# An attention and mixture-of-experts kernel: the first expert's weights loaded a group earlier, the k copies moved to ScalarE, the router two slots earlier

## The chip, the cores and the metric

The kernel runs on one core of one Trainium2 chip. A time is the device time of one execution in microseconds (us). The kernel before was run five times: 498.47, 499.37, 502.02, 503.82 and 508.04 us, median 502.02 us.

## What is computed

Two stages follow each other. The first is block-causal attention: 8 batches, 8 heads, 576 positions, head size 64. A query sees all keys of its own block of 64 positions and of the blocks before it. The second is a mixture of 8 experts on the 4608 rows that the attention gives, each row 512 wide.

```python
scores = scale * q @ k.T                       # masked by blocks of 64 positions
attn = softmax(scores)
x = (attn @ v) -> rows [4608, 512]             # heads side by side

noisy = x @ w_gate + log1p(exp(x @ w_noise)) * noise
top2 = two largest of 8 per row;  top2_w = softmax of those two
for e in range(8):
    for k in range(2):
        rows = top2[:, k] == e
        out[rows] += top2_w[rows, k] * (relu(x[rows] @ w1[e]) @ w2[e])   # w1 512x1024, w2 1024x512
```

## The kernel before

**Attention in groups and slots.** The batches are worked on in four groups of two (g = 0 to 3). A group has 26 score units (UG = 26), and a unit is one slot of a schedule written out by hand: `at(slot, fn, ...)` hangs a piece of work on a slot, and `run(u)` emits what hangs on slot u after the unit's own score matmuls (L288, L299) and their exponential on ScalarE (L291, L302). Each engine does its instructions in the order in which they are emitted. Two PSUM buffers hold scores (`sc_ps`), two the attention outputs and the router's products (`av_ps`), two the transposes (`tr_ps`).

- `load_qk` (L200, L202), `load_v` (L210): rows of q, k and v, fp32 in memory and bf16 in SBUF, by GpSimd's DMA queue.
- `transpose_qk`: TensorE transposes a chunk of q or k into PSUM (L250, L252), and VectorE copies it to SBUF: q at L255 in straight order, k at L257 with a strided read, since the columns of k are wanted in token order. A group has six k chunks: four of 128x1024 and two of 64x512. After chunk 0 VectorE also copies one block of 64 columns within SBUF (L261).
- `av_tile`: the product with v (L325, L336), and its division by the sum on VectorE (L339, L340) into `xr`.
- `x_transpose` (L354, copied at L355), then `router`, a chain of 15 steps: logits (L365), an exponential and a logarithm on ScalarE (L369 to L371), the two largest of eight on VectorE (L375 to L395), ranks by a scan (L399 to L406), two matmuls for the counts (L411, L412, into an `av_ps` buffer) and the row's place in its expert's list (L416 to L456). The slots of the steps are in the list `rsl`.
- `scatter`: 18 indirect DMAs per group, on GpSimd (L474), that write each row of `xr` to two places of the table `xd[half]`. Groups 0 and 1 make half 0, groups 2 and 3 half 1. They start at slot `r1` after the group's end.

The work of a group's second part runs beside the scores of the next group. For group 3 it runs beside the first steps of the expert stage.

**Experts.** `SEQ` lists 16 batches b of (half, expert), each of up to 640 rows: first half 0 of experts 0 to 3, then half 1 of experts 0 to 3, then both halves of experts 4 to 7 in turn. `load_x` (L493) loads a batch's rows transposed by a DMA of the sync engine's queue (SP): into `xa` for b = 0, into one of three `xg` buffers after that. It waits for all 36 scatters of its half. `load_rec` (L500) loads what the router wrote beside each row. `layer1` (L548, Relu at L551) and `layer2` (L560) follow; the product of layer 2 goes, scaled, to a table in memory (L565, L566), or is added to the row that was gathered from there (`gather`, L587; L569) and scattered to the output (L571).

**Queues.** SP's queue does, in order: the noise, eight DMAs that clear part of `xd[0]`, eight that clear part of `xd[1]` (`clear_x`, L619, each held back until the exponential of a named slot), `load_x(0)`, `load_rec(0)`, `load_x(1)`, `load_x(2)`, and then writes and loads of the experts. GpSimd's queue does all other transfers in order: rows of q, k and v, scatters, weights and gathers. The DMAs of this queue take eight completion semaphores in turn, and each waits until the DMA eight places before it has landed. Weights come from `load_w`: with k = 0 to 3 it loads half of w1 (k = 0, 1) or half of w2 (k = 2, 3) of one expert, 512 KB each as bf16 (L227). The schedule of this part is, in the kernel before:

```python
at(3 * UG + 12, load_x, 0)
at(3 * UG + 12, load_rec, 0)
...
at(UG + 4, clear_x, 0, UG + 3)
at(3 * UG + 4, clear_x, 1, 3 * UG + 3)
for k in range(4):
    at(3 * UG + (2, 5, 8, 11)[k], load_w, wE, 0, k)
    at(3 * UG + (14, 17, 20, 23)[k], load_w, wE, 1, k)
```

Of the kernel before, what the change touches and what calls it, by code (L numbers as in the profile page):

```python
# [11 lines left out]
AF = mybir.ActivationFunctionType  # L12
# [7 lines left out]
def kernel(  # L20
# [12 lines left out]
    nc = tc.nc  # L33
# [30 lines left out]
    UG = 2 * UN  # L64
# [32 lines left out]
    wE = main.enter_context(tc.tile_pool(name="wE", bufs=2))  # L97
# [132 lines left out]
    def transpose_qk(g, nm, ch):  # L230
        dst = qT if nm == "q" else kT
        tp = tr_ps.tile([P, 1024], BF16, tag="tr")


        if ch in (0, 1, 2, 3):
            raw = raws[(g, nm, ch)]
            p0, p1, c0, nb = 0, P, ch * 1024, 16
        else:
            raw = raws[(g, nm, 4)]
            p0 = 0 if ch == "4A" else 64  # L240
            p1, c0, nb = p0 + 64, 4 * 1024, 8
        n = nb * 64
        if nm == "q":
            to = tp[:, 0:n].rearrange("p (b r j) -> p b r j", b=nb, r=8)
        else:
            to = tp[:, 0:n].rearrange("p (r b j) -> p b r j", b=nb, r=8)
        for r in range(8):
            if nb == 16:
                for hf in range(2):
                    nc.tensor.transpose(to[64 * hf:64 * hf + 64, :, r, :], raw[:, hf, r * 64:(r + 1) * 64], ident)  # L250
            else:
                nc.tensor.transpose(to[p0:p1, :, r, :], raw[p0:p1, 0, r * 64:(r + 1) * 64],  # L252
                                    ident[p0:p1, p0:p1])
        if nm == "q":
            nc.vector.tensor_copy(dst[p0:p1, c0:c0 + n], tp[p0:p1, 0:n])  # L255
        else:
            nc.vector.tensor_copy(dst[p0:p1, c0:c0 + n].rearrange("p (b j r) -> p b j r", b=nb, j=8),  # L257
                                  tp[p0:p1, 0:n].rearrange("p (r b j) -> p b j r", r=8, b=nb))
        if ch == 0:

            nc.vector.tensor_copy(dst[64:128, 72 * 64:73 * 64], dst[64:128, 0:64])  # L261
# [343 lines left out]
    def at(slot, fn, *args):  # L605
        todo.setdefault(slot, []).append((fn, args))
# [75 lines left out]
    for ch in ("4B", 0):  # L682
        for nm in "qk":
            transpose_qk(0, nm, ch)
    at(0, transpose_qk, 0, "q", 1)
    at(0, transpose_qk, 0, "k", 1)

    for g in range(NG):
        s0 = g * UG
        if g + 1 < NG:  # L690
            early = 5 if g else 0
            at(s0 + 13 - early, transpose_qk, g + 1, "q", "4B")
            at(s0 + 13 - early, transpose_qk, g + 1, "k", "4B")
            at(s0 + 13, transpose_qk, g + 1, "q", 0)
            at(s0 + 15, transpose_qk, g + 1, "k", 0)
            at(s0 + 24, transpose_qk, g + 1, "q", 1)
            at(s0 + 25, transpose_qk, g + 1, "k", 1)
            at(s0 + 18, load_qk, g + 1, (2, 3))
            at(s0 + 11, load_v, g + 1)
        if g + 2 < NG:  # L700
            at(s0 + 20, load_qk, g + 2, (4, 0, 1))
        at(s0 + 3, transpose_qk, g, "q", 2)
        at(s0 + 5, transpose_qk, g, "k", 2)
        at(s0 + 10, transpose_qk, g, "q", 3)
        at(s0 + 12, transpose_qk, g, "k", 3)
        at(s0 + 17, transpose_qk, g, "q", "4A")
        at(s0 + 18, transpose_qk, g, "k", "4A")
        for i in range(TG):
            at(s0 + UN + 2 + i, av_tile, g, 0, i)
        r0 = s0 + UG  # L710
        if g < 2:
            for i in range(TG):
                at(r0 + 1 + i, av_tile, g, 1, i)
            for j in range(5):
                at(r0 + min(4 + 2 * j, 11), x_transpose, g, j)
            rsl = [12, 13, 14, 15, 16, 17, 18, 19, 20, 21, 21, 22, 22, 23, 23]
            r1 = 24
        elif g == 2:
            for i in range(TG):
                at(r0 + 1 + 2 * i // 3, av_tile, g, 1, i)  # L720
            for j in range(5):
                at(r0 + (3, 5, 6, 7, 8)[j], x_transpose, g, j)
            rsl = [9, 9, 10, 11, 12, 13, 14, 14, 15, 16, 16, 17, 17, 18, 18]
            r1 = 19
        else:
            for i in range(TG):
                at(r0 + i // 2, av_tile, g, 1, i)
            for j in range(5):
                at(r0 + 2 + j, x_transpose, g, j)
            rsl = [7, 7, 8, 9, 9, 10, 11, 11, 12, 13, 13, 14, 14, 15, 15]  # L730
            r1 = 16
        for j in range(RSTEPS):
            at(r0 + rsl[j], router_step, g)
        for j in range(2 * TG):
            at(r0 + r1 + (2 * j // 3 if g else j), scatter, g, j)
    at(3 * UG + 12, load_x, 0)
    at(3 * UG + 12, load_rec, 0)
    at(6, setup_consts)
    at(7, sort_nz, 0)
    at(8, transpose_nz, 0)  # L740
    at(9, sort_nz, 1)
    at(11, transpose_nz, 1)
    at(UG + 4, clear_x, 0, UG + 3)
    at(3 * UG + 4, clear_x, 1, 3 * UG + 3)
    for k in range(4):
        at(3 * UG + (2, 5, 8, 11)[k], load_w, wE, 0, k)
        at(3 * UG + (14, 17, 20, 23)[k], load_w, wE, 1, k)
    for u in range(NG * UG):
        score_unit(*divmod(u, UG))
        run(u)  # L750
# [61 lines left out]
    with tc.If(rs["over"] > 0):  # L812
# [4 lines left out]
        for g in range(NG):  # L817
# [5 lines left out]
            for idx in range(TG):  # L823
                for p0, tok in token_blocks(g, idx):
                    nc.sync.dma_start(out=token_order(tok_w[tok:tok + 64, :]), in_=wd[p0:p0 + 64, g, idx, :])
                    nc.sync.dma_start(out=token_order(tok_s[tok:tok + 64, :]),
                                      in_=slots[p0:p0 + 64, g * TG + idx, 0:1])
        for half in range(NH):
            with tc.For_i(half * TH * P, (half + 1) * TH * P, P) as r0:
# [6 lines left out]
                    out=xo.bitcast(I32), out_offset=None, in_=xd[half].bitcast(I32),  # L836
                    in_offset=bass.IndirectOffsetOnAxis(ap=sidx, axis=0),
                    bounds_check=XR - 1, oob_is_err=False)
                tp = tr_ps.tile([P, 1024], BF16, tag="tr")
# [53 lines left out]
```

## Time and profile before

| What | Value |
|---|---|
| median of five runs | 502.02 us |
| the profiled execution: its time, its span in the trace | 498.71 us, 496.8 us |
| granted TensorE clock, mean over the span | 0.902 of full speed |
| TensorE matmuls busy (PE) | 421.4 us, 85% |
| ScalarE busy (ACT) | 238.5 us, 48% |
| VectorE busy (DVE) | 182.6 us, 37% |
| GpSimd busy (POOL, its DMA issues among it) | 252.8 us, 51% |
| first matmul of the experts (L548) starts at | 176.72 us |

How to read it: the profile is of one execution. The span runs from its first to its last instruction; the rest of the 498.71 us lies around it. Times of single instructions are counted from the span's start. A busy TensorE is not a TensorE at its peak, since matmuls overlap. PE is the TensorE matmul, PEld its weight load, SPq the sequencer of the sync engine that issues DMAs. A group of instructions is named by its source line, engine, operation and tiles (out<-in). "Idle before" is the time in which the engine had nothing to do just ahead of the instruction, and the arrow tells what it then waited for. Busy shares are averages over two unlike stages: up to about 165 us attention, then the experts.

### The profile page before, as it was taken

The page shows a single profiled execution, that of the slowest core. Times are in us where ns is not written, and L with a number is a line of the kernel's source. Part 1 is how long each engine was busy: PE and PEld are TensorE (multiplying, and loading weights), DVE is VectorE, ACT ScalarE, POOL GpSimd, SP SyncE. Part 2 cuts the span into 40 slices and gives each one's busy share as a digit, 9 for nine tenths or more (in the row PEclk, how much of TensorE's full clock was granted, in tenths as well). Part 3 has the DMA queues.
Part 4 walks back from the last instruction along what each step waited for, and adds up shares of the span by engine and source line. Part 5 has one row for each costly group of instructions (what it writes and reads, how often), then busy time and mean ns, then how long its engine had stood idle before and what let it go on. Part 6 is the DMA issues. An engine that isn't in the chain of part 4 may idle for free.

```text
span 496.8 us, 9869 instructions
## 1 busy us (share of the span) xinstructions
PE 421.4 (85%) x3936; PEld 258.8 (52%) x3952; DVE 182.6 (37%) x552; ACT 238.5 (48%) x319; POOL 252.8 (51%) x297
## 2 busy tenths in 40 slices
PE   3788968988868279998383999999989999999994
PEld 2456645664635156555151556655645655665561
DVE  3687898788876238300100301011011022023112
ACT  1658776566475114545050545545535554554330
POOL 8775384786785253277330301234452463475553
PEclk9959997778875579999695999999999999999999
DMA  8999999399779999957696586887999984695232
GB/s 134 162 136 148 206 144 170 107 114 145 192 177 181 155 157 211 211 142 200 149 155 102 128 186 128 159 157 186 143 215 192 216 222 113 138 184 178 81 119 96
DMA packets 134763, 78.68 MB, mean 158 GB/s; under 512 B 96130, under 2 KB 124548, under 8 KB 134709
## 3 DMA queue, kind: packets, MB, share of 16 engines
q0 software_dynamic: 70496, 55.79, 74.2%
q1 hardware_dynamic: 64212, 22.18, 22.8%
q8 instruction: 33, 0.54, 0.5%
q14 instruction: 22, 0.17, 0.1%
HBM read 68.28 MB, written 33.13 MB: 204 GB/s over the span
## 4 chain that ended last, share of the span: by engine, by line
PE 30%; issue 25%; POOL 14%; DMA 14%; DVE 14%; ACT 1%; POOLq 1%; ACTq 0%; DVEq 0%
PE yp L560 11%; PE hp L548 10%; POOL yg L587 5%; DMA xa<-xd 5%; POOL out_dram L571 5%; DMA xd<-xr,slots 4%; PE tp L250 3%; DVE hq L257 3%; DVE xr L340 2%; DMA xg<-xd 2%; POOL xd L474 2%; PE sc L288 2%; PE av L325 2%; DMA yg<-yd,orow 2%; PE av L336 1%
## 5 line engine op out<-in xcount | busy, mean ns | idle before, releaser
L560 PE MATMUL yp<-w2sb,hq 128*128 128x512 bf16 x624 | 144.0, 386 | 13.1 <-DVE yo L569 11.6
L548 PE MATMUL hp<-xg,w1sb 128*128 128x320 bf16 x960 | 134.2, 300 | 8.7 <-DMA xg<-xd 8.7
L548 PEld LDWEIGHTS <-w1sb 128*128 128x128 bf16 x1024 | 100.6, 99 | 62.1 <-DMA xd<-xr,slots 11.3
L551 ACT ACTIVATE hq<-hp 128x640 bf16<-128x640 f32 x128 | 90.1, 704 | 89.0 <-PE hp L548 89.0
L569 DVE SCALAR_TENSOR_TENSOR yo<-yp,wrow,yg 128x512 f32<-128x512 f32 x46 | 34.4, 751 | 248.8 <-ACT ysb L565 181.5
L291 ACT ACTIVATE esc<-sc 128x1024 bf16<-128x1024 f32 x96 | 94.3, 1025 | 60.7 <-PE sc L288 59.7
L560 PEld LDWEIGHTS <-hq 128*128 128x128 bf16 x640 | 63.4, 99 | 89.4 <-issue 21.0
L474 POOL DMA_INDIRECT xd<-xr,slots x72 | 71.5, 993 | 53.5 <-issue 14.9
L571 POOL DMA_INDIRECT out_dram<-yo,trow x46 | 46.6, 1014 | 96.6 <-DVE yo L569 88.7
L565 ACT ACTIVATE ysb<-yp,wrow 128x512 bf16<-128x512 f32 x70 | 48.1, 687 | 90.7 <-PE yp L560 90.7
L587 POOL DMA_INDIRECT yg<-yd,orow x46 | 47.2, 1026 | 52.0 <-ACT hq L551 40.4
L288 PE MATMUL sc<-hq 64*128 64x512 bf16 (+4 forms) x320 | 44.0, 350 | 5.1 <-ACT esc L291 3.5
L325 PE MATMUL av<-vt,esc 128*128 128x65 bf16 x640 | 36.5, 215 | 11.5 <-DVE xr L340 10.0
L325 PEld LDWEIGHTS <-esc 128*128 128x128 bf16 x640 | 28.9, 111 | 25.3 <-DVE xr L340 14.5
L210 POOL DMA_DIRECT2D vt<-in_v_dram x40 | 33.7, 872 | 13.5 <-PE av L336 8.5
L340 DVE TENSOR_TENSOR xr<-av,rden 128x256 bf16<-128x256 f32 x72 | 30.6, 424 | 2.5
L250 PE MATMUL tp<-ident,t 128*64 128x128 bf16 x512 | 26.2, 262 | 2.2 <-DMA t<-in_q_dram 2.0
L257 DVE COPY hq<-tp 128x1024 bf16<-128x1024 bf16 (+1 forms) x24 | 25.6, 1066 | 4.3 <-PE tp L250 3.6
L250 PEld LDWEIGHTS <-t 128*64 128x64 bf16 x512 | 20.2, 135 | 7.7 <-issue 3.8
L339 DVE RECIPROCAL rden<-av 128x4 f32<-128x4 f32 x72 | 12.6, 175 | 30.1 <-PE av L325 21.5
L548 PE MATMUL hp<-xa,w1sb 128*128 128x320 bf16 x64 | 11.2, 325 | 11.2 <-DMA xa<-xd 11.2
L288 PEld LDWEIGHTS <-hq 64*128 64x128 bf16 x320 | 12.3, 100 | 15.5 <-issue 8.3
(126 smaller groups left out, 239.4 us busy)
## 6 DMA issues: line engine op xcount, KB each, us to landing
yd<-ysb SPq DMA_DIRECT2D x70, 128.0 KB, 2.4
w1sb<-in_moe_w_dram POOLq DMA_DIRECT2D x12, 512.0 KB, 6.8
w2sb<-in_moe_w_dram POOLq DMA_DIRECT2D x12, 512.0 KB, 9.1
t<-in_q_dram POOLq DMA_DIRECT2D x16, 256.0 KB, 7.3
t<-in_k_dram POOLq DMA_DIRECT2D x16, 256.0 KB, 8.0
vt<-in_v_dram POOLq DMA_DIRECT2D x32, 128.0 KB, 7.9
xd<-zero SPq DMA_DIRECT2D x16, 132.0 KB, 4.6
w1sb<-in_moe_w_dram POOLq DMA_DIRECT2D x2, 1024.0 KB, 10.5
```

The lines of the kernel that those rows point to most:

```text
L250: nc.tensor.transpose(to[64 * hf:64 * hf + 64, :, r, :], raw[:, hf, r * 64:(r + 1) * 64], ident)
L288: nc.tensor.matmul(out=sc[:, hf, off:off + z - a], lhsT=kT[sl, c0 + jt * P:c0 + jt * P + P], rhs=qT[sl, c0 + a:c0 + z], start=True, stop=True)
L291: ins = nc.scalar.activation(out=esc[:, hh, :, piece * 512:(piece + 1) * 512], in_=sc, func=AF.Exp, scale=scale)
L325: nc.tensor.matmul(out=av[:, hh, :], lhsT=esc[:, hh, hf, c:c + P], rhs=vb[:, 4 * hf + jt, h, :], start=(jt == 0), stop=(jt == ib))
L340: nc.vector.tensor_tensor(out=xr[:, idx, st * SET * D:(st + 1) * SET * D].rearrange("p (h d) -> p h d", h=SET), in0=av[:, :, 0:D], in1=rde ...
L474: ins = nc.gpsimd.indirect_dma_start(out=xd[half].bitcast(I32), out_offset=bass.IndirectOffsetOnAxis(ap=slots[:, g * TG + idx, i:i + 1], a ...
L548: nc.tensor.matmul(out=hp[:, n, 0:NW], lhsT=w1sb[:, db, fb * P:(fb + 1) * P], rhs=xgs[b][:, db, n * NW:(n + 1) * NW], start=(db == 0), sto ...
L551: ins = nc.scalar.activation(out=hs[b][:, fb, :].rearrange("p (n w) -> p n w", n=2), in_=hp[:, :, 0:NW], func=AF.Relu)
L560: nc.tensor.matmul(out=yp, lhsT=hs[b][:, fb, c * P:(c + 1) * P], rhs=w2sb[:, fb, :], start=(fb == 0), stop=(fb == FB - 1))
L565: nc.scalar.activation(out=ysb, in_=yp, func=AF.Copy, scale=w)
L571: ins = nc.gpsimd.indirect_dma_start(out=out, out_offset=bass.IndirectOffsetOnAxis(ap=trow[half][:, e, c:c + 1], axis=0), in_=yo, in_offse ...
L587: ins = nc.gpsimd.indirect_dma_start(out=yg, out_offset=None, in_=yd[half][0:e * CAP, :], in_offset=bass.IndirectOffsetOnAxis(ap=orows[hal ...
```

## The change

Four edits of the schedule and one of an engine.

- The copy of a k chunk out of PSUM (L257) is an activation with the function Copy on ScalarE in place of a copy on VectorE.
- The router steps of groups 0 and 1 are drawn together and end two slots earlier, and their scatters start two slots earlier (`r1` 24 becomes 22). In group 2 four steps move forward by one slot; its `r1` stays.
- The weights of expert 0 are hung on slots 4, 6, 8, 10 of group 2 in place of 2, 5, 8, 11 of group 3; those of expert 1 one slot earlier in group 3.
- `load_x(0)` moves from slot 12 to 11 of group 3, `load_rec(0)` from 12 to 14.
- The clears of half 1 move from slot 4 of group 3 to slot 4 of group 2.

```diff
         if nm == "q":
             nc.vector.tensor_copy(dst[p0:p1, c0:c0 + n], tp[p0:p1, 0:n])
         else:
-            nc.vector.tensor_copy(dst[p0:p1, c0:c0 + n].rearrange("p (b j r) -> p b j r", b=nb, j=8),
-                                  tp[p0:p1, 0:n].rearrange("p (r b j) -> p b j r", r=8, b=nb))
+            nc.scalar.activation(out=dst[p0:p1, c0:c0 + n].rearrange("p (b j r) -> p b j r", b=nb, j=8),
+                                 in_=tp[p0:p1, 0:n].rearrange("p (r b j) -> p b j r", r=8, b=nb), func=AF.Copy)
...
-            rsl = [12, 13, 14, 15, 16, 17, 18, 19, 20, 21, 21, 22, 22, 23, 23]
-            r1 = 24
+            rsl = [12, 12, 13, 14, 14, 15, 16, 17, 18, 19, 19, 20, 20, 21, 21]
+            r1 = 22
         elif g == 2:
...
-            rsl = [9, 9, 10, 11, 12, 13, 14, 14, 15, 16, 16, 17, 17, 18, 18]
+            rsl = [9, 9, 10, 11, 12, 12, 13, 13, 15, 16, 16, 17, 17, 18, 18]
             r1 = 19
...
-    at(3 * UG + 12, load_x, 0)
-    at(3 * UG + 12, load_rec, 0)
+    at(3 * UG + 11, load_x, 0)
+    at(3 * UG + 14, load_rec, 0)
...
-    at(3 * UG + 4, clear_x, 1, 3 * UG + 3)
+    at(2 * UG + 4, clear_x, 1, 2 * UG + 3)
     for k in range(4):
-        at(3 * UG + (2, 5, 8, 11)[k], load_w, wE, 0, k)
-        at(3 * UG + (14, 17, 20, 23)[k], load_w, wE, 1, k)
+        at(2 * UG + (4, 6, 8, 10)[k], load_w, wE, 0, k)
+        at(3 * UG + (13, 16, 19, 22)[k], load_w, wE, 1, k)
```

In the order of the instructions that follows, SP's queue is the same as before. On GpSimd's queue the four DMAs of expert 0's weights stand behind the 9th, 11th, 13th and 15th scatter of group 0, ahead of group 3's v rows; the 18 scatters of group 1 follow each other with nothing between; and the first two DMAs of expert 1's weights come right behind them. On ScalarE the 24 copies stand between the exponentials. VectorE's copy of 64 columns at L261 stays, and waits, for k, on ScalarE.

## Prediction

> **What bounds the kernel now.** First the rows of 40 slices (12.4 us each).
>
> ```profile
> PE   3788968988868279998383999999989999999994
> ...
> PEclk9959997778875579999695999999999999999999
> DMA  8999999399779999957696586887999984695232
> ```
>
> From slice 22 (273 us) on TensorE is full; nothing in the diff touches that stage. Before it I see attention at 8 to 9 tenths and three holes, in slices 13, 19 and 21. Beside the first hole DMA stands at 9 for five slices (149 to 211 us), while slice 7 (87 to 99 us) has DMA at 3. Next TensorE's waits by what ended them, first over the span, then for 0 to 166 us:
>
> ```profile
> PE yp L560 <- DVE yo L569: 11.6, 2, 9.6
> ...
> PE hp L548 <- DMA xa<-xd: 11.2, 1, 11.2
> ...
> PE hp L548 <- DMA xg<-xd: 8.7, 1, 8.7
> ```
>
> ```profile
> PE av L325 <- DVE xr L340: 10.0, 13, 1.6
> ...
> PE sc L288 <- ACT esc L291: 3.5, 8, 0.8
> PE pp L411 <- DVE xr L316: 3.2, 1, 3.2
> PE pp L411 <- DVE xr L340: 2.6, 2, 1.7
> PE tp L639 <- DVE xa L632: 2.4, 1, 2.4
> ```
>
> The three holes are 11.2, 9.6 and 8.7 us. In attention TensorE waits for VectorE 23.7 us in all (these rows with 1.6, 1.1, 1.5 and 1.3 of smaller ones), for ScalarE 4.0. The chain of work that ended last gives the first hole its cause:
>
> ```profile
> 140.75 5.09 DMA xd<-xr,slots
> 152.58 24.01 DMA xa<-xd
> 176.72 2.29 PE hp L548 x8
> ```
>
> The experts' first rows (xa) are asked for at 152.58 us, when the last scatter of group 1 has landed, and need 24.0 us; the page's DMA issues give 8.1 for the other fifteen such loads. GpSimd's timeline says what stands in front of them:
>
> ```profile
> 145.69 0.84 POOL L227 DMA_DIRECT2D w2sb<-in_moe_w_dram  x1
> 146.83 1.00 POOL L474 DMA_INDIRECT xd<-xr,slots  x1 [0.30 <-issue]
> 147.83 0.82 POOL L227 DMA_DIRECT2D w2sb<-in_moe_w_dram  x1
> 148.62 1.49 POOL L227 DMA_DIRECT2D w1sb<-in_moe_w_dram  x2
> ```
>
> Four 512 KB weight loads within 7 us of the request, and the last scatter among them.
>
> **What the Trainium skill says.** "DMA: Bandwidth & Descriptors", section "Issuing engines are not separate DMA queues": transfers from SP and GpSimd run on the same 16 DMA engines and interleave. The trace agrees: SP's load took 24.0 us beside GpSimd's weights, 8.1 without. The same page, "Queues, rings and completion order": each engine goes round the queues with work, packet by packet; so a load on SP's queue should not wait for all that GpSimd queued, only share with it. "TensorE: Matmul & The Clock Gate", Part 1: TensorE falls to half clock after about 3.4 us idle and comes back after as much sustained work. The windows agree roughly: 0.50 from 144 us, behind a 3.24 us gap at 142.7, until 180 us.
>
> **The change, part by part.** Sums are against the profiled execution (498.7 us, span 496.8).
>
> *k copies to ScalarE.* VectorE loses 24 copies: L257 has 25.6 us busy at 1066 ns. ScalarE gains 16 of 128x1024 and 8 of 64x512. The trace has no such strided read on ScalarE. Nearest row: L291, 128x1024 from PSUM, 1025 ns. "ScalarE: Activation LUTs" (What ACT_TABLE_LOAD costs) gives 186 ns + 0.833 ns an element, so an estimated 0.61 us for 512. Sum 16 x 1.03 + 8 x 0.61 = 21.4 us; if the stride halved the rate, about 39 us. I take 21.4[...]. What it frees: I went through TensorE's gaps in its timeline and kept those where a k copy stands in VectorE's queue just ahead of what TensorE waits for. At 23.6, 31.9, 125.7, 146.0 and 154.6 us each gives back the copy, 1.2; at 85.9 the gap, 1.15; at 57.4 0.6; at 74.2 and 114.0 0.8 each. Sum 9.35 us. The gaps at 69.2 (1.56) and 109.1 (1.33) I do not count: the L261 copy there now waits for ScalarE, which is in the middle of five exponentials in a row (64.0 to 68.7 us), and the division at L339 and L340 is queued behind it, and TensorE's next av_tile behind that. Charged back: where exponentials come back to back a copy delays the next scores. ScalarE was busy 99.7 of 165.5 us, so most copies fall into idle time; I charge a fifth of 21.4, 4 us. Net gain 5.4, bounds 0 and 10. If the gap at 142.7 shrinks enough for the clock to hold, up to 4 us more; not counted.
>
> *Router two slots earlier; weights out of the scatter chain.* A slot is 39 us / 26 = 1.5 us, so group 1's scatters start 3 us earlier than at 122.3, and earlier by what attention gained by then (4): 115.3 us. VectorE's router steps crowd into fewer slots, where the k copies left room. 18 scatters at 1.285 us from start to start are 23.1 us; before, three weight loads stood among them and the last ended at 147.8. Now 138.4. Landing took 152.6 - 147.8 = 4.8 us before; taken again, xa is asked for at 143, not 152.6.
>
> *xa.* TensorE gets to the first L548 at 165.6 - 5.4 = 160. So xa has 17 us. Expert 0's weights (2 MB) are gone from in front of it; the two w1 loads of expert 1 still are. Between 8.1 and 24.0 us I take 14 to 16: landed by 159, no wait. Gain 11.2 us.
>
> *Expert 0's weights and clears in group 2.* They are issued at about 86 to 95 us, into slice 7 where DMA stood at 3. They cost nothing while that idle share covers them. What is queued behind them on GpSimd's queue: group 3's v rows, its second and third q and k chunks, group 1's scatters. The 4 loads take 6.8 or 9.1 us each to land; all overlapped they are done at 95 + 9 = 104, one after another at 86 + 31.8 = 118. The q chunk was issued at 115.3, lands in 7.3, and is used at 128.7: 6 us to spare. With the lower end nothing waits, with the upper TensorE would wait for q about 8 us. I take nothing, since the eight clears (132 KB, 4.6 us to land) are small and the windows from 84 to 100 us show a DMA share of 0.30.
>
> *Slots of load_x(0) and load_rec(0).* SP's order is the same in both programs, and load_x waits for scatters, not for its slot: nothing.
>
> *After 177 us.* The holes at 234 (a gather queued behind group 3's scatters and a 1 MB weight load) and at 260 us (a load that SP reaches only behind layer 2's writes) hang on steps of the expert stage itself; they move forward with it and keep their 9.6 and 8.7 us. I take off 0.6 for the xg loads and expert 1's weights, which are now needed sooner.
>
> Sum: 5.4 + 11.2 - 0.6 = 16.0. The profiled execution would be at 482.7; the median shown lies 3.3 above it, so 502.0 - 16.0 = **486**.
>
> **The rivals.** *The copies give nothing.* TensorE and ScalarE are tied by two score buffers, so a relieved VectorE may only uncover ScalarE. For it: the rows of five exponentials, and ScalarE's waits for scores go with it. Against: nine gaps that a k copy ends. Only the 11.2 us remain: 491.
>
> *DMA sets the pace.* If 149 to 211 us is bound by bytes and not by the order of requests, all that follows can move only by the bytes that left. Of expert 0's weights 1.05 MB (the two w2 loads) were still in flight with xa; at the 159 GB/s of the windows from 149 to 176 us that is 6.6 us: 495. For it: DMA at 9 in five slices. Against: those windows moved 159 GB/s, others in the trace over 260. The late q chunk above belongs here too.
>
> *ScalarE becomes the bound* (slower). The place: attention, in the order exponential, k copy, exponential, with scores waiting for their buffer. The price is up to 21.4 us, or 39 at half rate. Since 11.2 us of waiting for xa take up a longer attention, the kernel is slower only once attention grows by over 11.2, by over 1% at 16.2 us, that is with three quarters of the copies' time on the path at full rate, or two fifths at half rate. Half of 39 on the path is 19.5 - 11.2 = 8 longer: 510. Against: ScalarE has 66 idle us in attention.
>
> **How the numbers follow.** Forecast 0.45 (479 to 492), copies give nothing 0.22 (491, 487 to 495), DMA sets the pace 0.22 (495, 491 to 502), ScalarE the bound 0.11 (510, 500 to 520). About 1% (497 to 507) is what a measurement of this kernel can tell from no change. Faster by over 1%: the first two nearly whole and 0.15 of the third, 0.81. Within 1%: the rest of the third and a little of the last, 0.09. Slower 0.10. The range 478 to 500 holds the first two and most of the third.
>
> **What would show it.** After, the wait PE hp L548 <- DMA xa should be gone or under 3 us and the first L548 start at 158 to 163 us; xa's load should start near 143 and take under 18 us. In 0 to 166 us TensorE's waits for VectorE should fall from 23.7 to some 14, those for ScalarE rise from 4.0 by at most 4. L257 should stand under ACT at about 1.03 us for 1024. The waits of 9.6 and 8.7 should remain. I am wrong if L250 waits for q or k of group 3, if the copies take 2 us, or if the gain at the first L548 is larger than that at 273 us, which would mean that it is given back between.

## The result, and the profile after

The changed kernel takes 497.30 us (median of 41 runs, 490.09 to 512.61) beside 500.72 us for the kernel before (78 runs, 494.94 to 514.28). The ratio of their times is 0.9922, 95% interval 0.9900 to 0.9943: 3.9 us faster, where 16 were forecast. Some runs of most kernels come out slower than the rest, so the ratios count the faster runs alone; the traces of e4, e5, e7 and e9 below are of slower runs, and nothing but the length of the end is read from one of them by itself. The profiled execution took 494.35 us, span 492.6 us, clock 0.897.

The rows of 40 slices (12.3 us each), the kernel after:

```profile
PE   3789878897978899992929999999899999999980
...
PEclk9957995986795699997868999999999999999996
DMA  9999999599739999688793976769998959594330
```

Two holes are left of the three (slices 18 and 20, counted from 0 as in the prediction); the one at the experts' start is closed. New is the last slice, where PE stands at 0; DMA stands at 3, 3 and 0 in the last three. TensorE's waits over the span, the kernel after (us in total, times, longest):

```profile
PE yp L560 <- DVE yo L569: 11.3, 2, 9.7
PE sc L288 <- ACT esc L291: 10.1, 14, 1.4
PE hp L548 <- DMA xg<-xd: 8.8, 1, 8.8
PE av L325 <- DVE xr L340: 8.2, 12, 1.3
```

The 11.2 us for xa have no row any more; 9.7 and 8.8 stayed, as forecast. In attention (0 to 166 us) the waits for VectorE fell from 23.7 to 12.7 us (8.2, 1.7, 1.6, 1.0, 0.2), those for ScalarE rose from 4.0 to 12.3 (10.1, 1.1, 0.6, 0.5). The chain of work has no xa in it now, and the first expert matmul stands at 166.8 us in it, not 176.7:

```profile
165.10 1.72 PE av L325 x28
166.82 2.13 PE hp L548 x8
```

GpSimd's timeline of the kernel after shows where the queue's time went:

```profile
104.30 0.83 POOL L227 DMA_DIRECT2D w2sb<-in_moe_w_dram  x1
105.44 1.02 POOL L474 DMA_INDIRECT xd<-xr,slots  x1 [0.30 <-issue]
107.37 2.73 POOL L210 DMA_DIRECT2D vt<-in_v_dram  x3 [0.92 <-DMA xd<-xr,slots]
...
119.84 0.77 POOL L200 DMA_DIRECT2D t<-in_q_dram  x1
...
124.08 1.06 POOL L474 DMA_INDIRECT xd<-xr,slots  x1 [0.30 <-issue]
```

Expert 0's weights were issued from 94.1 to 105.1 us, group 3's v rows until 116.9, its q and k until 123.8, and group 1's scatters began at 124.08, not at 115.3 as forecast and later than before (122.31). They then ran back to back and ended at 147.0 (before 147.8).

Everything behind moved forward: the last output scatter starts 11.8 us earlier. First the kernel before, then the kernel after:

```profile
491.19 0.98 POOL L571 DMA_INDIRECT out_dram<-yo,trow  x1 [0.75 <-DVEq L812]
```

```profile
479.41 0.98 POOL L571 DMA_INDIRECT out_dram<-yo,trow  x1 [0.74 <-DVEq L812]
```

But the span is only 4.2 us shorter. The rest is behind that scatter, in the program's last instructions. Again before, then after (form: line, queue, instruction, count; ns min/median/max; first and last start):

```profile
L812 POOLq INC_SWDGE_SEM  x1: 480/480/480, 494.3 to 494.3; - x1
...
L888 POOLq DRAIN  x3: 51/103/1212, 494.8 to 496.6; - x3
```

```profile
L812 POOLq INC_SWDGE_SEM  x1: 1970/1970/1970, 482.4 to 482.4; - x1
...
L888 POOLq DRAIN  x3: 51/103/7337, 484.4 to 492.3; - x3
```

The longest DRAIN of GpSimd's queue takes 1.2 us before and 7.3 us after; the step ahead of it, INC_SWDGE_SEM, takes 0.48 and 1.97. From the last scatter's end to the end of the span it is 4.6 us before and 12.2 us after: 7.6 us of the gain are lost where no engine computes any more. I call this stretch "the end" below.

### The profile page after: what moved, and what is told of

It reads as the page before. It is cut to its first block, busy times and chain, and to the rows that moved or that the text cites. A ratio compares the mean times of both kernels' runs of the same rounds, so it can differ in the third digit from the quotient of the medians.

```text
span 492.6 us, 9869 instructions
## 1 busy us (share of the span) xinstructions
PE 422.3 (86%) x3936; PEld 258.9 (53%) x3952; DVE 161.1 (33%) x528; ACT 257.1 (52%) x343; POOL 253.1 (51%) x297
## 4 chain that ended last, share of the span: by engine, by line
PE 33%; issue 23%; POOL 15%; DMA 11%; DVE 9%; ACT 6%; POOLq 1%; DVEq 0%; ACTq 0%
PE yp L560 10%; PE hp L548 8%; POOL yg L587 5%; POOL out_dram L571 5%; ACT esc L291 4%; PE av L325 3%; PE av L336 3%; PE sc L288 3%; PE tp L250 2%; DMA xg<-xd 2%; DMA xd<-xr,slots 2%; DVE xr L340 2%; DMA vt<-in_v_dram 2%; DMA yg<-yd,orow 2%; DMA yd<-ysb 1%
## 5 line engine op out<-in xcount | busy, mean ns | idle before, releaser
L560 PE MATMUL yp<-w2sb,hq 128*128 128x512 bf16 x624 | 143.2, 385 | 12.6 <-DVE yo L569 11.3
L291 ACT ACTIVATE esc<-sc 128x1024 bf16<-128x1024 f32 x96 | 94.5, 1033 | 28.3 <-PE sc L288 27.8
L288 PE MATMUL sc<-hq 64*128 64x512 bf16 (+4 forms) x320 | 45.4, 359 | 11.4 <-ACT esc L291 10.1
L257 ACT ACTIVATE hq<-tp 128x1024 bf16<-128x1024 bf16 (+1 forms) x24 | 21.2, 882 | 15.0 <-PE tp L250 7.9
L288 PEld LDWEIGHTS <-hq 64*128 64x128 bf16 x320 | 12.7, 101 | 22.0 <-issue 14.5
L255 DVE COPY hq<-tp 128x1024 bf16<-128x1024 bf16 (+1 forms) x24 | 14.4, 599 | 14.9 <-PE tp L250 13.3
```

The costliest lines, as they stand in the source:

```text
L288: nc.tensor.matmul(out=sc[:, hf, off:off + z - a], lhsT=kT[sl, c0 + jt * P:c0 + jt * P + P], rhs=qT[sl, c0 + a:c0 + z], start=True, stop=True)
L291: ins = nc.scalar.activation(out=esc[:, hh, :, piece * 512:(piece + 1) * 512], in_=sc, func=AF.Exp, scale=scale)
L560: nc.tensor.matmul(out=yp, lhsT=hs[b][:, fb, c * P:(c + 1) * P], rhs=w2sb[:, fb, :], start=(fb == 0), stop=(fb == FB - 1))
```

## The experiments

Each ratio is against the kernel before on the same chip. e9 to e16 ran on chips where that takes 500 to 501 us, as in the first measurement; e1 to e8, e17 and e18 on chips where it takes 548 to 557 us, with a TensorE clock of 0.84 to 0.88 in the traces, against 0.89 to 0.92. I call the first the quick chips. The two groups are not mixed below; on the slower chips the changed kernel itself was not run, and the kernel before was timed but not traced. "Attention ends" is the start of the last exponential (L302) in ScalarE's timeline.

**e1 to e4: parts of the change (before at 555.6 us).** e1 is the kernel before with the k copies on ScalarE; e2 the kernel before with the weights' slots and the clears; e3 and e4 are the changed kernel without the copies and without weights and clears:

```diff
 e1 (to before)
-            nc.vector.tensor_copy(dst[p0:p1, c0:c0 + n]...
+            nc.scalar.activation(out=dst[p0:p1, c0:c0 + n]... func=AF.Copy)
 e2 (to before; e4 is the reverse, to after)
+    at(2 * UG + 4, clear_x, 1, 2 * UG + 3)
+        at(2 * UG + (4, 6, 8, 10)[k], load_w, wE, 0, k)
+        at(3 * UG + (13, 16, 19, 22)[k], load_w, wE, 1, k)
 e3 (to after)
+            nc.vector.tensor_copy(dst[p0:p1, c0:c0 + n]...
```

> The kernel before with one edit of the change: the k copies on ScalarE. Two questions: do the copies shorten attention, and is the tail (from the end of GpSimd's last output scatter to the end of the span: 4.6 us before, 12.2 us after) tied to the kernel. Theory 1 (copies are neutral, ScalarE's waits take the place of VectorE's; the tail is drawn anew in each execution): first L548 ready within 1.5 us of 165.5, wait for xa 9 to 12 us, ratio 0.995 to 1.005, tail anywhere from 4 to 13 us. Theory 2 (the tail grows when the work ends earlier): same wait for xa, tail 4 to 6 us. Theory of the prediction (copies give 5 us of attention, which the wait for xa hides): attention ends at 160, wait 15 us.

> The kernel before with the DMA edits alone: expert 0's weights and half 1's clears in group 2, expert 1's weights one slot earlier; router and copies as before. Theory 1 (the weights alone remove the wait for xa): wait for xa 0 to 4 us, first L548 at 165 to 170 us, ratio 0.985 to 0.995, tail anywhere from 4 to 13 us. Theory 2 (the tail grows when the work ends earlier): the same wait, but a tail of 9 to 13 us, so ratio 0.99 to 1.0. Rival (it needs the router's two slots): wait for xa 6 us or more.

> The changed kernel with the k copies back on VectorE. Theory 1 (copies neutral): first L548 within 2 us of 166.6 us, ratio 0.985 to 0.997, tail anywhere from 4 to 13 us. Theory 2 (the tail grows when the work ends earlier): tail 9 to 13 us again. Rival (crowded router steps need the room on VectorE): attention ends 3 us or more later than 166.6, with waits of L411 for VectorE above 6 us.

> The changed kernel with expert 0's weights, expert 1's weights and the clears back where they were in the kernel before; copies on ScalarE and the router two slots earlier stay. Theory 1 (the weights made the wait for xa): wait for xa 5 to 10 us, ratio 0.995 to 1.003, tail anywhere from 4 to 13 us. Theory 2 (the tail grows when the work ends earlier): tail 4 to 7 us. Rival (the earlier router alone is enough): wait under 3 us and first L548 at 168 us or before.

| run | ratio (95%) | the end, us | longest drain, us |
|---|---|---|---|
| e1 | 1.0140 (1.0014 to 1.0265) | 4.8 | 1.21 |
| e2 | 1.0201 (1.0120 to 1.0283) | 12.7 | 7.42 |
| e3 | 1.0316 (1.0243 to 1.0389) | 12.5 | 7.34 |
| e4 | 1.0108 (1.0060 to 1.0155) | 5.0 | 0.97 |

Both of my first theories of the end fell, that its length is drawn anew in each execution and that it grows when the work ends earlier: e2 and e3 end late and have the long end, e1 and e4 the short one, with values that repeat to some tens of ns. It comes with the move of the weights and the clears, which e2 and e4 move together; no run moves the clears alone. The times missed all expectations upward.

**e5 to e8: which part of the move, and e1 and e2 again (before at 548.2 us).** e5 puts expert 1's pieces back, e6 moves expert 0's by one slot; e7 is the kernel of e1, e8 that of e2.

```diff
 e5 (to after)
-        at(3 * UG + (13, 16, 19, 22)[k], load_w, wE, 1, k)
+        at(3 * UG + (14, 17, 20, 23)[k], load_w, wE, 1, k)
 e6 (to after)
-        at(2 * UG + (4, 6, 8, 10)[k], load_w, wE, 0, k)
+        at(2 * UG + (5, 7, 9, 11)[k], load_w, wE, 0, k)
```

> The changed kernel with expert 1's four pieces back at slots 14, 17, 20 and 23 of group 3; expert 0's pieces stay in group 2. Theory Q (the long end comes from the order in which transfers stand in GpSimd's queue, so that the whole queue ends in another position; when the work ends plays no part): the drain at the end is either that of the kernel before (1.2 us, with 0.48 us for the step ahead of it, 4.6 us after the last output scatter) or that of the changed kernel (7.3, 1.97, 12.2), nothing between, and which of them it is says whether it hangs on expert 1's place or on expert 0's. Rival M (the length of the end grows with how early expert 0's weights stand in the queue): 7.3 us here. The start of the expert stage stays where the changed kernel has it (within 2 us) in both; with a short end the ratio to the kernel before is some 0.978, with a long one 0.992.

> The changed kernel with expert 0's four pieces each one slot later in group 2 (5, 7, 9, 11): on GpSimd's queue the first three pieces and the fourth each stand behind one more row scatter, and nothing else moves. Theory Q (order in the queue): the end is again one of the two lengths, 4.6 or 12.2 us after the last output scatter, and may be either, because so small a shift already moves the position of the pieces. Rival M (expert 0's weights stand early): 12.2 us, unchanged. The front: first matmul of the experts at 166 to 168 us if the chip is like the one of the changed kernel's profile; ratio 0.978 with the short end, 0.992 with the long one.

> The kernel before with the k copies on ScalarE and nothing else. The prediction's term: attention 5.4 us shorter, of which the wait for xa then eats what it can, so 0.5 to 5 us gained, ratio 0.990 to 0.999. Rival (what the profile after says: VectorE's relief comes back as waits for ScalarE at the scores): attention no shorter, first expert matmul at 176 to 178 us as before, ratio 0.998 to 1.004. The end is short (4.6 us after the last output scatter) in both, since no transfer changes its place.

> The kernel before with the weights' slots and the clears moved, copies and router as they were. If the transfers alone carry the front's gain, the first expert matmul comes 9 to 11 us earlier than before and the wait for xa is gone; the end is long (12.2 us after the last output scatter), so the ratio is 0.992 to 0.996. If copies and router are needed for it (rival), the first expert matmul gains under 5 us and the ratio is 1.00 to 1.01.

e5: 1.0152 (1.0019 to 1.0286), e6: 1.0312 (1.0253 to 1.0372), both with a drain of 7.34 us: the long end does not hang on expert 1's slots, so expert 0's place is left, or the clears; both theories allowed that. e7: 0.9985 (0.9939 to 1.0031), end short; it is e1's kernel and does not repeat e1's loss, and its ratio lies in the ranges of both theories, so it decides nothing between them; e8: 1.0277 (1.0192 to 1.0362), end long. Both expectations of e8 are missed. In the traces of these chips attention ends at 184.6 to 192.7 us and xa has been asked for since 159 to 167 us, so TensorE has no wait for xa that could be removed (e1, with the weights at their old place, asks at 166.4 and starts the experts at 191.4 without a wait). What is left of the weights' move there is the long end, 7.6 us or 1.4%, and some loss that I did not trace.

**e9 to e12: the end by itself, and both kernels again (before at 500.5 us).** e9 and e10 are the changed kernel with one and with three transfers more on GpSimd's queue, late in the expert stage, into a tile that nobody reads. e11 is the kernel before, e12 the changed kernel.

```diff
 e10 (to after; e9 with range(1))
             if (b, j) in WL:
                 load_w(*WL[b, j])
+            if (b, j) == (11, 1):
+                for i in range(3):
+                    nc.gpsimd.dma_start(out=spare[:, i], in_=moe_w1[0][0:4 * P, 0:4].rearrange("(n p) c -> p n c", p=P))
```

> The changed kernel with one small transfer more on GpSimd's queue, late in the expert stage (512 pieces of 8 bytes into a spare tile; nobody reads it). Theory Q (the end's length is the position at which the queue stands when the program ends): the drain changes though nothing that matters was moved: away from 7.3 us by some 2 to 3 us, in either direction, or back to a small value if the position wraps; the step ahead of it changes with it in the ratio seen so far (1.97 to 7.34, 0.48 to 1.21: some 4.1 us of drain for each us of the step). Rival M (the early place of expert 0's weights makes the end long): 7.3 and 1.97 us, unchanged. The time itself moves by the change in the end only, 1 us at most for the issue.

> As the run with one such transfer, with three (1536 pieces). Theory Q: the drain differs from 7.3 us and from that of the run with one; if the length falls with each by the same step, three of them bring it under 2 us and the end from 12.2 to some 5 us, and the kernel is about 7 us faster than the changed kernel on the same chip; if it rises, over 9 us. Rival M: 7.3 us.

> The kernel before itself, for a trace of it on the chip of these runs. All theories: ratio 1.00 within its interval, the drain 1.2 us and the end 4.6 us after the last output scatter. If the chip is like that of the first runs (before at 540 to 570 us), the stretch up to the first expert matmul shows how much of the difference to the 496.8 us span lies in attention (estimate from the run with the copies alone: 12 to 18 us) and how much behind it.

> The changed kernel itself on the chip of these runs. If what was measured at 0.992 holds whatever the chip's pace: ratio 0.985 to 1.000. If the gain hangs on the pace of the chip (the parts of the change were 1.01 to 1.03 on chips where the kernel before takes 550 us): 1.01 to 1.03 there. The drain is 7.3 us in both.

e12: 0.9934 (0.9902 to 0.9966), e11: 0.9997 (0.9969 to 1.0025), as expected; both drains as in the first traces, 7.34 and 1.21 us. e9: 0.9984 (0.9953 to 1.0016), with a drain of 7.42 us, so 0.08 us longer and not 2 to 3 as Theory Q had it. Its ratio is 0.005 above e12's with the same end; I have no cause for that, and the intervals overlap. e10: **0.9798** (0.9739 to 0.9858), 10.1 us faster than the kernel before. Its last output scatter and its last instructions:

```profile
482.07 0.98 POOL L572 DMA_INDIRECT out_dram<-yo,trow  x1 [0.75 <-DVEq L816]
```

```profile
L816 POOLq INC_SWDGE_SEM  x1: 460/460/460, 485.5 to 485.5; - x1
...
L892 POOLq DRAIN  x3: 51/103/1130, 486.0 to 487.7; - x3
```

The last output scatter is no earlier than in the changed kernel (479.41 and 479.55 us), and the program ends 5.0 us after it, not 12.2 and 12.5. So the long end is a cost by itself of some 7 us (7.2 to 7.5 in the traces, 6.8 between the ratios of e12 and e10), and it can be had back without touching the work. Rival M is refuted: expert 0's weights stand where the change put them. Three transfers brought the end to the 5 us that Theory Q named, but not by equal steps, since the first changed nothing.

**e13 to e16: the copies, the router, and the end turned round (before at 501.2 us).** e13 is the kernel of e1, e14 that of e3, on another chip. e15 is the changed kernel with the router's slots of before. e16 is the kernel before with the three transfers of e10.

```diff
 e15 (to after)
-            rsl = [12, 12, 13, 14, 14, 15, 16, 17, 18, 19, 19, 20, 20, 21, 21]
-            r1 = 22
+            rsl = [12, 13, 14, 15, 16, 17, 18, 19, 20, 21, 21, 22, 22, 23, 23]
+            r1 = 24
...
-            rsl = [9, 9, 10, 11, 12, 12, 13, 13, 15, 16, 16, 17, 17, 18, 18]
+            rsl = [9, 9, 10, 11, 12, 13, 14, 14, 15, 16, 16, 17, 17, 18, 18]
```

> The kernel before with the k copies on ScalarE, on another chip than the first time. Theory A (ScalarE takes the place of VectorE: it has 24 copies of 0.88 us more to do between the exponentials that TensorE's next scores wait for): TensorE's waits for VectorE in the first 162 us fall by some 11 us and those for ScalarE rise by 7 to 8, attention ends within 2 us of before, the wait for xa stays at 9 to 13 us, ratio 0.996 to 1.004. The prediction's theory (5.4 us off attention, TensorE waits for xa instead, xa asked earlier by part of it): last exponential of attention 4 to 6 us earlier, ratio 0.985 to 0.995.

> The changed kernel with the k copies back on VectorE. Theory A: no loss, ratio to the kernel before 0.990 to 0.997, first expert matmul within 2 us of the changed kernel's (162 to 167 us). The prediction's theory: 5 us slower than the changed kernel, ratio 1.00 to 1.005. The end is the long one (12.2 us) in both.

> The changed kernel with the router of groups 0 to 2 and the scatters of group 1 back at their slots of before. Theory B (GpSimd's queue, with expert 0's weights, the v rows and the t loads ahead of them, lets group 1's scatters start no earlier than 122 to 124 us whatever the router does): xa is asked within 2 us of the changed kernel's 146.7 to 148.6 us, no wait for xa over 2 us, ratio 0.990 to 0.998. The change's own idea (two slots sooner, some 2 to 4 us): xa asked at 151 us or later, a wait for xa of 2 to 5 us comes back, ratio 0.998 to 1.005.

> The kernel before with the three small transfers late in the expert stage. If they shift the position at which GpSimd's queue ends, and it can fall either way: the drain either stays near 1.2 us with a step of tens of ns (ratio 0.998 to 1.003), or falls into the long form, 7 us and more (ratio 1.012 to 1.018). If they cure an end that expert 0's early place makes long: it stays at 1.2 us and can't go long. Nothing else moves by over 1 us.

e13: 0.9885 (0.9844 to 0.9926). e14: 1.0008 (0.9978 to 1.0038). Theory A falls on both: the copies alone bring 5.8 us (501.2 x 0.0115), and without them the changed kernel has lost its gain, 0.0074 against e12, some 3.7 us. ScalarE's part of Theory A is seen in e13 too (waits for scores 8.8 us against 3.5 before), but it does not eat the gain. The 5.8 us are near the forecast's 5.4, but they are not the same gain. Attention ends 4.3 us earlier (156.5 against 160.8, the mean of three traces of the kernel before). The experts still wait 9.0 us for xa, so their start follows xa: it is asked for at 149.9 us and lands 18.6 us later, not at 152.6 and 24.0 later, and the first expert matmul stands at 168.65, 7.9 us earlier than the mean before. Why it lands sooner I did not trace. The last exponential in the kernel before and the changed kernel of the first profiles, then in e13 and in e15:

```profile
162.35 0.38 ACT L302 ACTIVATE esc<-sc 128x256 bf16<-128x256 f32 x1
```

```profile
163.61 0.38 ACT L302 ACTIVATE esc<-sc 128x256 bf16<-128x256 f32 x1
```

```profile
156.46 0.38 ACT L302 ACTIVATE esc<-sc 128x256 bf16<-128x256 f32 x1
```

```profile
155.54 0.38 ACT L302 ACTIVATE esc<-sc 128x256 bf16<-128x256 f32 x1
```

e15: 0.9915 (0.9883 to 0.9947), attention ends at 155.54 us, and the experts start at 162.56, in the changed kernel at 162.2 to 166.9, now behind a wait for xa:

```profile
146.47 7.50 SPq L493 DMA_TRANSPOSE xa<-xd  x1
```

```profile
162.56 2.31 PE L548 MATMUL hp<-xa,w1sb 128*128 128x320 bf16 x8 [3.81 <-DMA xa<-xd]
```

xa is asked for at 146.5 us with the router at its old slots, at 146.7 to 148.6 with the new ones (e12, after): Theory B holds, the router's move brings xa no earlier; its "no wait for xa over 2 us" does not, the wait is 3.8. And the move costs attention: it ends at 155.5 us without it and at 159.7 to 163.9 with it (after, e10, e12). The kernel's time is the same (0.9915 against 0.9934 in e12).

e16: 1.0030 (0.9996 to 1.0064). The drain became 2.11 us and the step ahead of it 0.69, between the two forms, which none of the expectations had. The same three transfers that cured the long end lengthen the short one (4.6 to 6.3 us), so they are no cure in themselves.

**e17 and e18: the router's move alone, and the changed kernel without it and without the long end (before at 556.6 us).** e17 is the kernel before with the changed kernel's router slots, e18 the kernel of e15 with the three transfers of e10.

> The kernel before with only the router of groups 0 to 2 and the scatters of group 1 at the changed kernel's slots. Theory R (the router's steps, two to a slot, sooner, hold attention up on VectorE and TensorE): the last exponential of attention at 163 to 166 us, 2 to 5 us later than the 159.1 to 162.4 us of three traces of before. The wait for xa shrinks by what attention loses and by what xa is asked sooner, so the first expert matmul hardly moves: ratio 0.995 to 1.006. The change's own idea (two slots sooner, so scatters and xa sooner, attention untouched): last exponential at 159 to 162.5 us, group 1's scatters from 116 to 119 us, xa asked at 146 to 149 us, ratio 0.985 to 0.993. A TensorE clock of 0.5 between 75 and 85 us is seen in every trace with the sooner router; if it is the router's doing it is here too.

> The changed kernel with the router at its old slots and the three small transfers late on GpSimd's queue. Theory: attention ends at 155 to 157 us, TensorE waits 3 to 6 us for xa (asked at 146 to 148 us, landed 162 to 164 us), so the first expert matmul stands at 162 to 164 us; the end is the short one (some 6 us after the last output scatter) if the position falls as it did with the router moved. Then the ratio is 0.970 to 0.980, span 484 to 488 us. If the position falls into the long form: 0.985 to 0.993. If the router's place is nothing (rival): 0.976 to 0.984 with attention at 160 to 164 us.

e17: 1.0151 (1.0067 to 1.0236), with attention ending at 188.97 us; e18: 1.0069 (1.0034 to 1.0104), with attention ending at 185.18 and a short end (drain 1.29 us). Both ratios lie outside all that was expected; the numbers were written for a quick chip, so the times do not answer to either theory. What can be compared is the ten traces of these chips: attention ends at 184.6 to 188.4 us with the old router slots (e1, e2, e7, e8, e18) and at 186.6 to 192.7 with the sooner ones (e3, e4, e5, e6, e17), means 186.0 and 190.0. A loss of about that size is there by the 60th of the 104 exponentials, early in group 2, when group 0's router has run at its new slots: with the sooner router the 60th starts at 95.3 to 97.5 us on the quick chips (after, e9, e10, e12, e14) and at 101.3 to 103.5 on the others, with the old slots at 90.4 to 94.0 (before, e11, e13, e15, e16) and 97.5 to 99.5. The means differ by 3.5 us on both kinds, and none of the twenty traces lies on the wrong side, with the copies or without, with the weights moved or not. Alone, the move is a loss of 1.5% on the slower chips (e17); alone on a quick chip it was not run.

## Why the forecast was wrong

Three terms failed: the request for xa at 143 us, which overlooked GpSimd's queue; the router's steps drawn together, which were taken to cost nothing; and the end, which was taken as fixed. The places, means of the traces on quick chips (before: first profile, e11, e16; changed: first profile, e12, e10; the end without e10 and e16):

| place | forecast | measured |
|---|---|---|
| attention ends (last exponential), moved by | -5.4 us | +1.6 (160.8 to 162.4) |
| xa asked for at | 143 us | 146.7 to 148.6 |
| first expert matmul, at | 160 us | 165.2, from 176.5 |
| last output scatter starts, moved by | -16.0 us | -11.7 (492.0 to 480.3) |
| the end | no change | +7.5 (4.8 to 12.3) |

Attention's end differs by 3 to 4 us between traces of one kernel (159.1 to 162.4 before, 159.7 to 163.9 changed), so its +1.6 says only that the 5.4 did not come.

**k copies: right in mechanism, near in size partly by luck, taken back by another step.** L257 stands under ScalarE at 1.03 us for 1024 (forecast 1.03) and 21.2 us in all (forecast 21.4); the stride did not halve the rate. "ScalarE: Activation LUTs" (What ACT_TABLE_LOAD costs), by which the 512-wide copy was priced at 0.61 us, agrees: these copies take 0.59 us in the mean. What the copies free and what they charge back were both put too small. In e13 the waits for VectorE fell by 11.1 us to 12.6 (forecast 14) and those for ScalarE rose by 6.4, not by at most 4; in the changed kernel the fall is 11.0 and the rise 8.3. The two errors have opposite signs, so the net, 4.3 us less attention in e13, came near 5.4.

**Router two slots earlier: two failures.** "So group 1's scatters start 3 us earlier ... 115.3 us" did not look at what GpSimd has in front of them. In the trace of the kernel before, the four q and k loads that stand ahead of these scatters begin at 115.32 us themselves, and only the 4.05 us behind them were free:

```profile
115.32 0.78 POOL L200 DMA_DIRECT2D t<-in_q_dram  x1
...
117.51 0.75 POOL L200 DMA_DIRECT2D t<-in_k_dram  x1
122.31 1.05 POOL L474 DMA_INDIRECT xd<-xr,slots  x1 [4.05 <-ACT esc L302]
```

The change puts expert 0's four loads ahead of all this, and these in turn stand behind scatters of group 0: they were issued from 94.1 to 105.1 us, where the prediction had 86 to 95. With v rows that wait for their buffers and the q and k loads, the queue reached group 1's scatters at 124.08 us in the changed kernel and at 121.94 in e15 with the old slots, in both directly behind the last of those loads. They ended at 147.0, not 138.4. And "VectorE's router steps crowd into fewer slots, where the k copies left room" was taken as free. It is the term that the sum lacked in attention: the copies' 4.3 us (160.8 to 156.5) are gone in the changed kernel and back in e15. That it is the router's move is shown by removing it (e15), and its place by all traces. By what means it costs is not shown. In the changed kernel TensorE runs at half clock (0.50) in that stretch; the windows from 75 to 85 us of the changed kernel and of e15, whose columns are sum, busy us of PE, PEld, DVE, ACT, POOL, then clock, DMA share and GB/s:

```profile
75.00:85.00 10.00, 8.47 (x108) 5.03 (x108) 7.36 (x32) 5.41 (x6) 5.60 (x8) 0.50 1.21 204
```

```profile
75.00:85.00 10.00, 8.43 (x148) 5.72 (x149) 8.84 (x37) 7.60 (x9) 4.21 (x6) 0.83 0.99 172
```

Equally busy, TensorE issued 108 matmuls in one and 148 in the other. But two of the three traces of before (e11, e16) have 0.57 and 0.52 there, and e8 with the old slots has 0.50, and they lose nothing like it, so the clock alone does not explain it, and it may be an effect as well as a cause. "TensorE: Matmul & The Clock Gate", section "A second HAM failure mode", tells of a clock that swings because TensorE idles briefly and often; the stretch in the changed kernel follows gaps of 1.34 and 0.86 us, the longest between 58 and 76 us, which fits that better than the 3.4 us of the page's Part 1 that the prediction leaned on. No run here separates the two.

**xa: the wait gone as forecast, the request late.** With the weights out of the way the wait of 11.2 us is gone, and in the changed kernel's traces the experts start 15.5 to 18.6 us after the request without a wait, so xa has landed by then. But it was asked for 3.7 to 5.6 us later than forecast, and how long the load takes is not settled. The rows of the DMA issues (the last number is us to landing) in e12 and in e15, where xa is asked for at 146.72 and 146.47 us:

```profile
xa<-xd SPq DMA_TRANSPOSE x1, 8.9
```

```profile
xa<-xd SPq DMA_TRANSPOSE x1, 16.0
```

In both, two loads of expert 1's w1 stand just ahead of the request, so these alone do not make it slow; the forecast had taken 14 to 16 us on their account. What differs is what comes next on GpSimd's queue: group 2's scatters. In e12 they start when the load has nearly landed, in e15, with attention ahead, beside it, and a w2 load of expert 1 follows them at 151.44 us. First e12, then e15:

```profile
154.57 1.06 POOL L474 DMA_INDIRECT xd<-xr,slots  x1 [7.91 <-ACT esc L291]
```

```profile
149.06 1.05 POOL L474 DMA_INDIRECT xd<-xr,slots  x1 [2.63 <-ACT esc L291]
```

That these scatters made the difference is argued from two traces, and no run tests it. What the trace of e15 shows is that an attention shorter by some 7 us meets an xa that lands at 162.5 us. So e15 starts the experts no sooner than e12 does: the two gains, 5.4 and 11.2, do not add as the sum had it, because the request had not moved to 143 us. With the 8.9 us of e12 it would have landed at some 155.4 us (an estimate, 146.5 + 8.9) and not have bound.

**After 177 us: the stage right, the end not looked at.** The stage kept its two waits and nothing was given back between, as the prediction's last check asks (10.1 us at the first expert matmul, 11.2 at the matmul behind the second hole, 11.8 at the last scatter). Nor did TensorE wait for q or k of group 3. The program's last 4.6 us were taken as fixed. They depend on what was issued on GpSimd's queue (e10), and on where transfers stood hundreds of microseconds earlier (e2, e8): +7.5 us. Of the 11.8 us missing (16.0 less 11.7 - 7.5), that is the larger part; the other 4.3 are missing at the first expert matmul already.

None of the rivals was the case. "The copies give nothing" looked right in the changed kernel's trace, where attention is no shorter; e13 refutes its reason. "DMA sets the pace" gave 495 (491 to 502), and 497.3 lies in that range, but by luck: the wait for xa is gone and the experts start 11.3 us earlier, where that rival gave 6.6, and what is missing went elsewhere. ScalarE did not become the bound: TensorE's waits for it rose by 8.3 us, not by the 16 and more that a slower kernel needed.

**What stays open.** What the end counts. "DMA: Bandwidth & Descriptors" (SWDGE vs HWDGE vs iDMA) says that GpSimd appends the descriptors of its DMAs to rings that the DMA engines empty, and that one queue is allocated for them. A place in such a ring is a natural reading, which no run here shows: the drain and the step ahead of it lie on one line over all runs (0.42 and 0.97, 0.46 and 1.13, 0.48 and 1.21, 0.50 and 1.29, 0.69 and 2.11, 1.97 and 7.34, 1.99 and 7.42 us; some 4.1 us per us), repeat to 0.1 us wherever the order on the queue is alike, and change when transfers are added. But one transfer added 0.08 us, three took 6.2 away, and the same three added 0.9 to the kernel before; I have no rule for that. Whether the clears take part, and what the drain waits for, is open too.

## What to carry to other kernels

Follow a moved instruction through everything that stands ahead of it on its queue: two slots in the program were worth nothing, because GpSimd's queue had no room to start the scatters sooner, and drawing its steps together cost attention some 3.5 us. Two gains that meet at one point (attention's end and xa's landing) are worth the later of the two, not their sum. And look at the span behind the last useful instruction before and after, since there 7.6 of 11.8 us were lost; three tiny transfers more on the queue (e10, 0.9798) had them back, but the same three made the end of the kernel before longer (e16), so this has to be tried on each kernel.

## What the runs showed of the hardware

The end of this program took 4.6 us (the kernel before) to 12.8 us (e8) after its last GpSimd DMA, by what was queued before and in which order. A copy of 128x1024 from PSUM on ScalarE with a strided read took 1.03 us (L257 after), as long as an exponential of that size with a plain read (1.025, L291 before). The load of xa took 8.9, 16.0, 18.6 and 24.0 us (e12, e15, e13, before), by what was in flight beside it or by something not traced. And the kernel before takes 500 to 502 us on some chips and 548 to 557 on others (clock in the traces 0.89 to 0.92 against 0.84 to 0.88). In no trace of the latter do the experts wait for xa, so a change that removes that wait has nothing to gain there: all ratios on them lie between 0.9985 and 1.0316, and the weights' move alone costs 2 to 2.8% (e2, e8).
